# A decode kernel with cached attention and a dense branch: weights on 128 partitions, keys loaded three pieces and transposed one piece ahead, last values in four loads, sums in PSUM

## The chip, the cores and the metric

One core of one Trainium2 chip. The metric is the device time of one execution in microseconds (us), the median of several runs; lower is better. The page of a profile shows one execution. Engines: TensorE (PE, matmuls; PEld, weight loads), VectorE (DVE), ScalarE (ACT), GpSimd (POOL), SyncE (SP, which issues the loads), and 16 DMA engines. In the built programs each of the five engines has a queue of instructions of its own.

## The reference

Two tokens (batch 2, one position, D = 448). x is normalised; one branch is attention over the last 4,096 positions of a cache (16 query heads, 8 key heads, head size 256), the other a dense layer with the mish function; both are added to x.

```python
xn = layernorm(x)
q = (xn @ wq)                                   # wq [448, 4096], 16 heads of 256
s = einsum("bhqd,bhkd->bhqk", q, k[last 4096]) * 256 ** -0.5
o = einsum("bhqk,bhkd->bhqd", softmax(s), v[last 4096])
out = x + o @ wo + mish(xn @ w1 + b1) @ w2      # wo [4096, 448], w1 [448, 1792], w2 [1792, 448]
```

The data are 67.1 MB of keys and values and 10.6 MB of weights, all in bf16, 77.67 MB together.

## The kernel before

The work is cut into 32 pieces: 8 key heads, 2 batch entries, 2 halves of the positions. A piece needs 1 MB of keys and 1 MB of values. For each piece VectorE transposes the keys (kt, read as four-byte words), TensorE makes the scores with a block-diagonal q (8 matmuls), ScalarE takes the exponential and its sum (rs), VectorE transposes the result (pT), TensorE multiplies by the values (32 small matmuls into o). After two pieces den sums rs over the partitions, rec is 1/den, oT is o times rec; after four, psA collects oT times wo.

```python
def scores(s):
    kt = kt_pool.tile([P, TH * Dh], BF16, tag="kt", name="kt")          # bufs=2
    nc.vector.transpose(out=kt[:].bitcast(FP32), in_=k_t.pop(s)[:].bitcast(FP32))
    ...                                            # 8 matmuls, then Exp into p, sum into rs
def values(s):
    nc.vector.transpose(out=pT[:], in_=p_t.pop(s)[:])
    ...                                            # 32 matmuls into o; after the second half:
    ...                                            # den <- rs, rec <- 1/den, oT <- o * rec
for s in range(NSTEP + 1):
    if s + 2 < NSTEP: load_k(s + 2)
    if s + 1 < NSTEP: load_v(s + 1)                # every fourth also loads a wo
    ...
    if s < NSTEP: scores(s)
    if s >= 1:    values(s - 1)
```

wq and w1 lie on 112 partitions (448 = 4 x 112), wq in two loads. The framework in which the kernel is written orders the instructions of each engine itself when the program is built. **The queues need not have the order of the source**, and the order of a built program can be listed.

The softmax here doesn't subtract the row's maximum and nothing guards it: scores larger than these inputs give would overflow.

Of the kernel before, what the change touches and what calls it, by code (L numbers as in the profile page):

```python
# [9 lines left out]
ALU = mybir.AluOpType  # L10
# [7 lines left out]
def kernel(  # L18
# [29 lines left out]
    NS = 4  # L48
    PD = D // NS
    NF = F // P  # L50
# [3 lines left out]
    assert Sq == 1 and D % NS == 0 and PD <= P and F % P == 0  # L54
# [8 lines left out]
    kt_pool = ctx.enter_context(tc.tile_pool(name="kt", bufs=2))  # L63
# [11 lines left out]
    b1_sb = consts.tile([P, NF], BF16)  # L75
    nc.scalar.dma_start(out=b1_sb[:, :], in_=B_b1.rearrange("(q c) -> q c", q=P))

    wq_sb = weights.tile([PD, NS, HqDh], BF16)
    wq_in = A_wq.rearrange("(p s) n -> p s n", s=NS)
    NG = 2  # L80
    HG = Hq // NG
    GW = HG * Dh
    for g in range(NG):
        nc.sync.dma_start(
            out=wq_sb[:, :, g * GW : (g + 1) * GW], in_=wq_in[:, :, g * GW : (g + 1) * GW]
        )
# [20 lines left out]
    for i in range(NW):  # L107
# [17 lines left out]
    xn_bf = consts.tile([Bsz, D], BF16)  # L125
    nc.vector.tensor_scalar(  # L126
        out=xn_bf[:],
        in0=x_bf[:],
        scalar1=mv[:, 0:1],
        scalar2=rstd[:],  # L130
        op0=ALU.subtract,
        op1=ALU.mult,
    )
    xnT_ps = ps_m.tile([P, NS, Bsz], BF16, tag="m", name="xnT_ps")
    xn_v = xn_bf[:, :].rearrange("b (p s) -> b s p", s=NS)
    for s in range(NS):
        nc.tensor.transpose(xnT_ps[0:PD, s, :], xn_v[:, s, :], ident[0:Bsz, 0:Bsz])  # L137
    xnT = consts.tile([PD, NS, Bsz], BF16)
    nc.vector.tensor_copy(out=xnT[:], in_=xnT_ps[0:PD, :, :])


    qrep = consts.tile([P, NB, Hq, NE, Bsz], BF16)
    wq_v = wq_sb[:, :, :].rearrange("p s (h m e) -> p s h e m", h=Hq, e=NE)

    def project(g):
        qT_ps = ps_m.tile([P, HG, NE, Bsz], FP32, tag="m", name="qT_ps")
        for hh in range(HG):
            for e in range(NE):
                for s in range(NS):
                    nc.tensor.matmul(  # L150
                        qT_ps[:, hh, e, :],
                        lhsT=wq_v[:, s, g * HG + hh, e, :],
                        rhs=xnT[:, s, :],
                        start=(s == 0),
                        stop=(s == NS - 1),
                    )
        qT = small.tile([P, HG * NE * Bsz], BF16, tag="qT", name="qT")
        nc.vector.tensor_copy(out=qT[:], in_=qT_ps[:].rearrange("p h e b -> p (h e b)"))  # L158
        qr_ps = ps_m.tile([P, NB, HG * NE * Bsz], FP32, tag="m", name="qr_ps")
        for b4 in range(NB):  # L160
            nc.tensor.matmul(
                qr_ps[:, b4, :], lhsT=spread[:, b4, :], rhs=qT[:], start=True, stop=True
            )
        nc.vector.tensor_copy(
            out=qrep[:, :, g * HG : (g + 1) * HG, :, :].rearrange("p n h e b -> p n (h e b)"),
            in_=qr_ps[:],
        )
# [3 lines left out]
    def build_q(i):  # L171
        kvh, b = heads[i]
        t = qdiag[i % NW]
        tv = t[:].rearrange("p (n e) c -> p n e c", e=NE)
        for j in range(NQ):
            rows = slice(j * Q, (j + 1) * Q)
            for e in range(NE):
                nc.gpsimd.tensor_copy(  # L178
                    out=tv[rows, :, e, j * Q : j * Q + rep],
                    in_=qrep[rows, :, kvh * rep : (kvh + 1) * rep, e, b],  # L180
                )


    w1_sb = weights.tile([PD, NS, F], BF16)
    w2_sb = weights.tile([P, NF, D], BF16)
    xb = consts.tile([Bsz, D], FP32)
    act_bf = consts.tile([P, NF, Bsz], BF16)

    def load_dense():
        nc.sync.dma_start(out=w1_sb[:], in_=B_w1.rearrange("(p s) n -> p s n", s=NS))  # L190
        nc.sync.dma_start(out=w2_sb[:], in_=B_w2.rearrange("(q c) d -> q c d", q=P))

    def dense_in():
        w1_v = w1_sb[:].rearrange("p s (q c) -> p s c q", c=NF)
        hT_ps = ps_m.tile([P, NF, Bsz], FP32, tag="m", name="hT_ps")
        for c in range(NF):
            for s in range(NS):
                nc.tensor.matmul(  # L198
                    hT_ps[:, c, :],
                    lhsT=w1_v[:, s, c, :],  # L200
                    rhs=xnT[:, s, :],
                    start=(s == 0),
                    stop=(s == NS - 1),
                )
        h_sb = consts.tile([P, NF, Bsz], FP32, name="h_sb")
        nc.vector.tensor_tensor(
            out=h_sb[:],
            in0=hT_ps[:],
            in1=b1_sb[:].unsqueeze(2).to_broadcast([P, NF, Bsz]),
            op=ALU.add,  # L210
        )
        u_sb = consts.tile([P, NF, Bsz], FP32, name="u_sb")
        nc.scalar.activation(out=u_sb[:], in_=h_sb[:], func=ACT.Exp)
        t_sb = consts.tile([P, NF, Bsz], FP32, name="t_sb")
# [3 lines left out]
        den = consts.tile([P, NF, Bsz], FP32, name="den_sb")  # L218
# [7 lines left out]
    def dense_out():  # L226
        psB = ps_m.tile([Bsz, D], FP32, tag="m", name="psB")
        for c in range(NF):
            nc.tensor.matmul(  # L229
                psB[:, :],  # L230
                lhsT=act_bf[:, c, :],
                rhs=w2_sb[:, c, :],
                start=(c == 0),
                stop=(c == NF - 1),
            )
        nc.vector.tensor_tensor(out=xb[:], in0=psB[:, :], in1=x_bf[:], op=ALU.add)
# [3 lines left out]
    k_t, v_t, p_t, wo_t = {}, {}, {}, {}  # L240
    psA = ps_a.tile([Bsz, D], FP32)
# [10 lines left out]
    def load_v(s):  # L252
# [4 lines left out]
        nc.sync.dma_start(out=t[:], in_=vin[:, half * TH : (half + 1) * TH, :])  # L257
        v_t[s] = t
        if half == NH - 1 and b == Bsz - 1:
            w = wo_pool.tile([P, rep, ND * D], BF16, tag="wo", name="wo")  # L260
            r0 = kvh * rep * Dh
            nc.sync.dma_start(
                out=w[:],
                in_=A_wo[r0 : r0 + rep * Dh, :].rearrange("(h p c) d -> p h (c d)", h=rep, p=P),
            )
            wo_t[kvh] = w

    def scores(s):
        i = s // NH
        kt = kt_pool.tile([P, TH * Dh], BF16, tag="kt", name="kt")  # L270
        nc.vector.transpose(out=kt[:].bitcast(FP32), in_=k_t.pop(s)[:].bitcast(FP32))  # L271
        ktv = kt[:].rearrange("p (t n c e) -> p n e t c", t=TH, n=NB, e=NE)
# [22 lines left out]
    def values(s):  # L295
# [7 lines left out]
        po = state["o", i]  # L303
        v = v_t.pop(s)
# [13 lines left out]
        rs = state.pop(("rs", i))  # L318
        den = ps_den.tile([P, rep], FP32, tag="den", name="den")
        for n in range(NH):  # L320
            nc.tensor.matmul(  # L321
                den[:],
                lhsT=rs[:, n : n + 1].to_broadcast([P, P]),
                rhs=hsel[:],
                start=(n == 0),
                stop=(n == NH - 1),
            )
        rec = small.tile([P, rep], FP32, tag="rec", name="rec")
        nc.vector.reciprocal(out=rec[:], in_=den[:])  # L329
# [12 lines left out]
        for h in range(rep):  # L342
            for c in range(ND):
# [4 lines left out]
                    start=(kvh == 0 and h == 0 and c == 0),  # L348
                    stop=(kvh == Hkv - 1 and h == rep - 1 and c == ND - 1),
                )  # L350

    load_k(0)
    load_k(1)
    load_v(0)
    project(0)
    build_q(0)
    build_q(1)
    for s in range(NSTEP + 1):
        if s + 2 < NSTEP:
            load_k(s + 2)  # L360
        if s + 1 < NSTEP:
            load_v(s + 1)
        if s == 3:
            load_dense()
# [46 lines left out]
```

## Time and profile before

| | before |
|---|---|
| median, range | 211.82 us, 209.85 to 212.22 (4 runs) |
| span of the profiled run | 211.8 us |
| TensorE, VectorE, ScalarE busy | 70%, 49%, 12% |
| read from memory | 77.67 MB, 367 GB/s over the span |

The prediction below shows the slices, the stretches and the end. Two more views. First the chain of work that ended last, summed by engine:

```profile
DMA 64%; PE 24%; DVE 9%; issue 1%; ACT 0%; SPq 0%; ACTq 0%
```

Second, two pieces in steady state from the timeline (start, duration, engine, line, operation, result and operands, count, and in brackets how long the engine had stood idle and what ended it):

```profile
133.92 0.70 DVE L299 STREAM_TRANSPOSE pT<-p 128x512 bf16<-128x512 bf16 x1
134.54 2.27 DVE L271 STREAM_TRANSPOSE kt<-k 128x2048 f32<-128x2048 f32 x1
136.87 3.48 PE L276 MATMUL sc<-kt,qdiag 128*128 128x512 bf16 x8 [2.69 <-DVE kt L271]
137.24 2.31 DVE L271 STREAM_TRANSPOSE kt<-k 128x2048 f32<-128x2048 f32 x1 [0.43 <-DMA k<-in_A_k_cache_dram]
...
141.37 1.89 PE L276 MATMUL sc<-kt,qdiag 128*128 128x512 bf16 x8
...
144.78 2.27 DVE L271 STREAM_TRANSPOSE kt<-k 128x2048 f32<-128x2048 f32 x1
```

VectorE does two key transposes in a row. The first waits behind pT, and its scores wait for it; the second is already done when its scores come. Those follow other work without a wait and took 1.89 us at a granted clock of 1.00; the eight that had waited 2.69 us took 3.48 us at a mean of 0.54. Two pieces take 144.78 - 134.54 = 10.2 us.

### The profile page before, as it was taken

Reading aid. Unit: us, or ns where it says so; the run is one execution under the profiler, and the core shown is the slowest. Engines: PE = TensorE matmul, PEld = TensorE weight load, DVE = VectorE, ACT = ScalarE, POOL = GpSimd, SP = SyncE. Lnnn points to the kernel's source line nnn. Section 1 sums busy time; section 2 is a strip of 40 time slices with the busy share of each in tenths; the row PEclk is TensorE's granted clock in tenths of the full one; section 3 lists DMA queues with packets and bytes.
Section 4 is the critical chain, followed back from the end, with each engine's and each line's share of the span. In section 5 each row is a group of like instructions: output and inputs, shape, how many; then the busy total and the mean of one; then the engine's idle time right before and its main releaser. Section 6 shows DMA issues by size and latency. Waiting matters only on the chain.

```text
span 211.8 us, 3784 instructions
## 1 busy us (share of the span) xinstructions
PE 148.2 (70%) x1586; PEld 80.4 (38%) x1586; DVE 103.9 (49%) x134; ACT 25.1 (12%) x68; POOL 26.7 (13%) x138
## 2 busy tenths in 40 slices
PE   1006486946869598858694969496949596878584
PEld 0006243513563354434343434353524343344342
DVE  5200847245124654556565555645555553656511
ACT  5000020101100111111111111111111111111110
POOL 7001520200200020112020202020202020000000
PEclk9999997678555967696969797978888857696966
DMA  5999999999999999999999999999999999999500
GB/s 152 281 278 381 416 421 421 408 342 227 330 409 421 411 418 421 421 404 422 422 415 411 420 415 421 409 419 419 421 407 419 416 421 412 421 416 420 215 7 0
DMA packets 12760, 77.90 MB, mean 368 GB/s; under 512 B 1364, under 2 KB 3416, under 8 KB 4312
## 3 DMA queue, kind: packets, MB, share of 16 engines
q1 hardware_dynamic: 12596, 77.67, 93.7%
q8 instruction: 12, 0.20, 0.4%
q10 hardware_dynamic: 148, 0.01, 0.1%
q14 instruction: 4, 0.03, 0.0%
HBM read 77.67 MB, written 0.00 MB: 367 GB/s over the span
## 4 chain that ended last, share of the span: by engine, by line
DMA 64%; PE 24%; DVE 9%; issue 1%; ACT 0%; SPq 0%; ACTq 0%
DMA k<-in_A_k_cache_dram 30%; DMA v<-in_A_v_cache_dram 29%; PE sc L276 15%; DVE kt L271 6%; DMA wq_sb<-in_A_wq_dram 5%; PE o L308 4%; PE psB L229 3%; DVE pT L299 2%; PE den L321 1%; PE psA L344 1%; DVE oT L333 0%; DVE res L379 0%; ACT p L286 0%; SPq L249 0%; DVE den_sb L222 0%
## 5 line engine op out<-in xcount | busy, mean ns | idle before, releaser
L276 PE MATMUL sc<-kt,qdiag 128*128 128x512 bf16 x256 | 91.0, 517 | 38.7 <-DVE kt L271 38.1
L271 DVE STREAM_TRANSPOSE kt<-k 128x2048 f32<-128x2048 f32 x32 | 72.8, 2285 | 10.3 <-DMA k<-in_A_k_cache_dram 10.1
L276 PEld LDWEIGHTS <-qdiag 128*128 128x128 bf16 x256 | 29.3, 123 | 82.4 <-issue 38.1
L178 POOL COPY qdiag<-qrep 32x8 bf16<-32x8 bf16 x128 | 22.9, 184 | 146.3 <-PE sc L276 116.2
L286 ACT ACTIVATE p<-sc 128x512 bf16<-128x512 f32 x32 | 19.1, 597 | 174.0 <-PE sc L276 174.0
L299 DVE STREAM_TRANSPOSE pT<-p 128x512 bf16<-128x512 bf16 x32 | 22.5, 704 | 31.6 <-ACT p L286 31.6
L308 PEld LDWEIGHTS <-v 128*128 128x128 bf16 x1024 | 31.7, 99 | 13.3 <-issue 10.3
L308 PE MATMUL o<-pT,v 128*128 128x2 bf16 x1024 | 30.6, 164 | 0.4 <-DVE rec L329 0.4
L333 DVE TENSOR_TENSOR oT<-o,rec 128x4 bf16<-128x4 f32 x16 | 2.6, 165 | 38.5 <-PE o L308 38.5
L321 PE MATMUL den<-hsel,rs 128*128 128x2 f32 x64 | 12.9, 273 | 0.1
L150 PE MATMUL qT_ps<-xnT,wq_sb 112*128 112x2 bf16 x128 | 3.9, 165 | 12.2 <-DMA wq_sb<-in_A_wq_dram 12.2
L321 PEld LDWEIGHTS den<-hsel,rs 128*128 128x128 f32 x64 | 10.2, 202 | 4.6 <-issue 2.7
L344 PE MATMUL psA<-wo,oT 128*2 128x448 bf16 x32 | 7.6, 362 | 2.1 <-DVE oT L333 2.1
L150 PEld LDWEIGHTS <-wq_sb 112*128 112x128 bf16 x128 | 3.6, 104 | 12.3 <-DMA wq_sb<-in_A_wq_dram 12.3
L158 DVE CAST qT<-qT_ps 128x32 bf16<-128x32 f32 x2 | 0.4, 190 | 13.9 <-PE qT_ps L150 13.9
L229 PE MATMUL psB<-w_sb,act_bf 128*2 128x448 bf16 x14 | 5.4, 574 | 1.8 <-DVE act_bf L224 1.8
L286 ACT ACTIVATION_READ_ACCUMULATOR p<-sc 128x1 f32 x32 | 6.2, 194 | 0.0
L198 PE MATMUL hT_ps<-xnT,w_sb 112*128 112x2 bf16 x56 | 3.5, 198 | 0.6 <-DMA w_sb<-in_B_w_dram 0.6
L137 PE MATMUL xnT_ps<-ident,xn_bf 2*112 2x2 bf16 x4 | 0.6, 243 | 4.6 <-DVE xn_bf L126 4.6
L198 PEld LDWEIGHTS <-w_sb 112*128 112x128 bf16 x56 | 3.4, 157 | 0.7 <-DMA w_sb<-in_B_w_dram 0.7
L344 PEld LDWEIGHTS <-oT 128*2 128x2 bf16 x32 | 2.0, 82 | 4.5 <-DVE oT L333 2.8
L229 PEld LDWEIGHTS <-act_bf 128*2 128x2 bf16 x14 | 1.6, 120 | 4.8 <-issue 3.0
(34 smaller groups left out, 18.5 us busy)
## 6 DMA issues: line engine op xcount, KB each, us to landing
k<-in_A_k_cache_dram SPq DMA_DIRECT2D x32, 1024.0 KB, 18.6
v<-in_A_v_cache_dram SPq DMA_DIRECT2D x32, 1024.0 KB, 18.6
wq_sb<-in_A_wq_dram SPq DMA_DIRECT2D x2, 1792.0 KB, 13.1
wo<-in_A_wo_dram SPq DMA_DIRECT2D x8, 448.0 KB, 18.6
w_sb<-in_B_w_dram SPq DMA_DIRECT2D x2, 1568.0 KB, 27.5
x_bf<-in_A_x_dram ACTq DMA_DIRECT2D x1, 1.8 KB
b_sb<-in_B_b_dram ACTq DMA_DIRECT2D x1, 3.5 KB, 5.8
out_dram<-res SPq DMA_DIRECT2D x1, 1.8 KB
```

What stands on the lines that cost most here:

```text
L150: nc.tensor.matmul(qT_ps[:, hh, e, :], lhsT=wq_v[:, s, g * HG + hh, e, :], rhs=xnT[:, s, :], start=(s == 0), stop=(s == NS - 1),)
L178: nc.gpsimd.tensor_copy(out=tv[rows, :, e, j * Q : j * Q + rep], in_=qrep[rows, :, kvh * rep : (kvh + 1) * rep, e, b],)
L198: nc.tensor.matmul(hT_ps[:, c, :], lhsT=w1_v[:, s, c, :], rhs=xnT[:, s, :], start=(s == 0), stop=(s == NS - 1),)
L229: nc.tensor.matmul(psB[:, :], lhsT=act_bf[:, c, :], rhs=w2_sb[:, c, :], start=(c == 0), stop=(c == NF - 1),)
L271: nc.vector.transpose(out=kt[:].bitcast(FP32), in_=k_t.pop(s)[:].bitcast(FP32))
L276: nc.tensor.matmul(psc[:], lhsT=qdiag[i % NW][:, n * NE + e, :], rhs=ktv[:, n, e, :, :], start=(n == 0 and e == 0), stop=(n == NB - 1 and ...
L286: nc.scalar.activation(out=p_sb[:], in_=psc[:].rearrange("p t c -> p (t c)"), func=ACT.Exp, scale=scale, accum_out=state["rs", i][:, s % N ...
L299: nc.vector.transpose(out=pT[:], in_=p_t.pop(s)[:])
L308: nc.tensor.matmul(po[:, c, :], lhsT=vv[:, t, c, :], rhs=pTv[:, t, 0:rep], start=(half == 0 and t == 0 and c == 0), stop=(half == NH - 1 a ...
L321: nc.tensor.matmul(den[:], lhsT=rs[:, n : n + 1].to_broadcast([P, P]), rhs=hsel[:], start=(n == 0), stop=(n == NH - 1),)
L333: nc.vector.tensor_tensor(out=oT[:, :, :, b], in0=po[:], in1=rec[:].unsqueeze(1).to_broadcast([P, ND, rep]), op=ALU.mult,)
L344: nc.tensor.matmul(psA[:, :], lhsT=oT[:, c, h, :], rhs=w[:, h, c * D : (c + 1) * D], start=(kvh == 0 and h == 0 and c == 0), stop=(kvh == ...
```

## The change

Its intent: fill the holes in the loads by using all 128 partitions for wq and w1 (each row of the matrix cut into two half-rows, 896 = 7 x 128), let TensorE never wait for kt by transposing keys one piece ahead, shorten the end by loading the last values in four parts and wo early, and gather x and the dense branch in the PSUM tile of the attention.

```diff
-    wq_sb = weights.tile([PD, NS, HqDh], BF16)            # PD = 112
+    wq_sb = weights.tile([P, NS, HW], BF16)               # P = 128, NS = 7, HW = half a row
+    wq_in = A_wq.rearrange("r (x n) -> (r x) n", x=NX).rearrange("(p s) n -> p s n", s=NS)
...                                                         # w1 alike; xs holds xn, split by half-row
-    kt_pool = ... bufs=2
+    kt_pool = ... bufs=3
...
+        n = LAST if s == NSTEP - 1 else 1                  # load_v: LAST = 4
+        for u in range(n): ...
+    def turn(s):                                           # the key transpose, taken out of scores
+        kt = kt_pool.tile([P, TH * Dh], BF16, tag="kt", name="kt")
+        nc.vector.transpose(out=kt[:].bitcast(FP32), in_=k_t.pop(s)[:].bitcast(FP32))
...                                                         # values: den and rec moved ahead of the 32 matmuls
+    KA, VA = 3, 1
+    for s in range(KA): load_k(s)
+    load_wo(0)
...
+    turn(0)
     for s in range(NSTEP + 1):
-        if s + 2 < NSTEP:
-            load_k(s + 2)
+        if s + KA < NSTEP:
+            load_k(s + KA)
...
+        if s + 1 < NSTEP:
+            turn(s + 1)
         if s < NSTEP:
             scores(s)
         if s >= 1:
             values(s - 1)
...
-    nc.vector.tensor_tensor(out=res[:], in0=psA[:, :], in1=xb[:], op=ALU.add)
+    nc.vector.tensor_copy(out=res[:, 0 : D // 2], in_=psA[:, 0 : D // 2])
+    nc.scalar.copy(out=res[:, D // 2 : D], in_=psA[:, D // 2 : D])
```

More of the change, by code (lines that the diff above doesn't have):

```diff
@@ L47 @@
     TH = T // NH
-    NS = 4
-    PD = D // NS
-    NF = F // P
+    NX = 2
+    NS = D * NX // P
+    HW = HqDh // NX
+    HF = F // NX
+    HH = Hq // NX
+    NF = HF // P
     ND = Dh // P
@@ L53 @@
     NE = 2
-    assert Sq == 1 and D % NS == 0 and PD <= P and F % P == 0
+    assert Sq == 1 and D * NX == NS * P and NS % 2 == 1 and HF % P == 0 and Hq % NX == 0
     assert TH * Q <= 512 and NB * NE * Q == Dh and ND == 2
@@ L62 @@
     v_pool = ctx.enter_context(tc.tile_pool(name="vv", bufs=6))
-    kt_pool = ctx.enter_context(tc.tile_pool(name="kt", bufs=2))
+    kt_pool = ctx.enter_context(tc.tile_pool(name="kt", bufs=3))
     p_pool = ctx.enter_context(tc.tile_pool(name="pp", bufs=2))
@@ L74 @@
     nc.scalar.dma_start(out=x_bf[:, :], in_=A_x.flatten_outer_dims())
-    b1_sb = consts.tile([P, NF], BF16)
-    nc.scalar.dma_start(out=b1_sb[:, :], in_=B_b1.rearrange("(q c) -> q c", q=P))
-    wq_sb = weights.tile([PD, NS, HqDh], BF16)
-    wq_in = A_wq.rearrange("(p s) n -> p s n", s=NS)
-    NG = 2
-    HG = Hq // NG
-    GW = HG * Dh
-    for g in range(NG):
-        nc.sync.dma_start(
-            out=wq_sb[:, :, g * GW : (g + 1) * GW], in_=wq_in[:, :, g * GW : (g + 1) * GW]
-        )
+    b1_sb = consts.tile([1, F], BF16)
+    nc.scalar.dma_start(out=b1_sb[:, :], in_=B_b1.rearrange("(o f) -> o f", o=1))
+    wq_sb = weights.tile([P, NS, HW], BF16)
+    wq_in = A_wq.rearrange("r (x n) -> (r x) n", x=NX).rearrange("(p s) n -> p s n", s=NS)
+    SC = NS // 2 + 1
+    nc.sync.dma_start(out=wq_sb[:, 0:SC, :], in_=wq_in[:, 0:SC, :])
+    nc.sync.dma_start(out=wq_sb[:, SC:NS, :], in_=wq_in[:, SC:NS, :])
     ident = consts.tile([P, P], BF16)
@@ L124 @@
     nc.vector.reciprocal(out=rstd[:], in_=rstd[:])
-    xn_bf = consts.tile([Bsz, D], BF16)
-    nc.vector.tensor_scalar(
-        out=xn_bf[:],
-        in0=x_bf[:],
-        scalar1=mv[:, 0:1],
-        scalar2=rstd[:],
-        op0=ALU.subtract,
-        op1=ALU.mult,
-    )
-    xnT_ps = ps_m.tile([P, NS, Bsz], BF16, tag="m", name="xnT_ps")
-    xn_v = xn_bf[:, :].rearrange("b (p s) -> b s p", s=NS)
-    for s in range(NS):
-        nc.tensor.transpose(xnT_ps[0:PD, s, :], xn_v[:, s, :], ident[0:Bsz, 0:Bsz])
@@ L138 @@
-    xnT = consts.tile([PD, NS, Bsz], BF16)
-    nc.vector.tensor_copy(out=xnT[:], in_=xnT_ps[0:PD, :, :])
-    qrep = consts.tile([P, NB, Hq, NE, Bsz], BF16)
-    wq_v = wq_sb[:, :, :].rearrange("p s (h m e) -> p s h e m", h=Hq, e=NE)
-    def project(g):
-        qT_ps = ps_m.tile([P, HG, NE, Bsz], FP32, tag="m", name="qT_ps")
-        for hh in range(HG):
+    xn_bf = consts.tile([Bsz, NS, P // 2, 2], BF16)
+    x_all = x_bf[:, :]
+    for r in range(2):
+        n = (NS + 1 - r) // 2
+        nc.vector.tensor_scalar(
+            out=xn_bf[:, r : NS : 2, :, :],
+            in0=bass.AP(
+                x_all.tensor,
+                x_all.offset,
+                [list(x_all.ap[0]), [1, n], [NS, P // 2], [(NS + r) // 2, 2]],
+            ),
+            scalar1=mv[:, 0:1],
+            scalar2=rstd[:],
+            op0=ALU.subtract,
+            op1=ALU.mult,
+        )
@@ new lines @@
+    xnT_ps = ps_m.tile([P, NS, Bsz], BF16, tag="m", name="xnT_ps")
+    for s in range(NS):
+        nc.tensor.transpose(
+            xnT_ps[:, s, :],
+            xn_bf[:, s, :, :].rearrange("b u o -> b (u o)"),
+            ident[0:Bsz, 0:Bsz],
+        )
+    odd = consts.tile([P, 2], FP32)
+    nc.vector.tensor_reduce(
+        out=odd[:],
+        in_=ident[:].rearrange("p (u o) -> p o u", o=2),
+        axis=AXIS.X,
+        op=ALU.add,
+    )
+    xs = consts.tile([P, NS, NX, Bsz], BF16)
@@ new lines @@
+    for par in range(2):
+        for x in range(NX):
+            which = (par + x) % 2
+            nc.vector.tensor_scalar(
+                out=xs[:, par : NS : 2, x, :],
+                in0=xnT_ps[:, par : NS : 2, :],
+                scalar1=odd[:, which : which + 1],
+                scalar2=None,
+                op0=ALU.mult,
+            )
+    ones = consts.tile([1, Bsz], BF16)
+    nc.vector.memset(ones[:], 1.0)
+    psA = ps_a.tile([Bsz, D], FP32)
+    nc.tensor.matmul(
+        psA[:, :],
+        lhsT=ident[0:Bsz, 0:Bsz],
+        rhs=x_bf[:, :],
+        start=True,
+        stop=False,
+        skip_group_check=True,
+    )
@@ L148, in project @@
+    qrep = consts.tile([P, NB, HH, NE, NX, Bsz], BF16)
+    wq_v = wq_sb[:, :, :].rearrange("p s (h m e) -> p s h e m", h=HH, e=NE)
+    def project():
+        qT_ps = ps_m.tile([P, HH, NE, NX * Bsz], FP32, tag="m", name="qT_ps")
+        for hh in range(HH):
             for e in range(NE):
@@ L151, in project @@
                         qT_ps[:, hh, e, :],
-                        lhsT=wq_v[:, s, g * HG + hh, e, :],
-                        rhs=xnT[:, s, :],
+                        lhsT=wq_v[:, s, hh, e, :],
+                        rhs=xs[:, s, :, :].rearrange("p x b -> p (x b)"),
                         start=(s == 0),
@@ L156, in project @@
                     )
-        qT = small.tile([P, HG * NE * Bsz], BF16, tag="qT", name="qT")
-        nc.vector.tensor_copy(out=qT[:], in_=qT_ps[:].rearrange("p h e b -> p (h e b)"))
-        qr_ps = ps_m.tile([P, NB, HG * NE * Bsz], FP32, tag="m", name="qr_ps")
+        n = HH * NE * NX * Bsz
+        qT = consts.tile([P, n], BF16, name="qT")
+        nc.vector.tensor_copy(out=qT[:], in_=qT_ps[:].rearrange("p h e c -> p (h e c)"))
+        qr_ps = ps_m.tile([P, NB, n], FP32, tag="m", name="qr_ps")
         for b4 in range(NB):
@@ L164, in project @@
         nc.vector.tensor_copy(
-            out=qrep[:, :, g * HG : (g + 1) * HG, :, :].rearrange("p n h e b -> p n (h e b)"),
-            in_=qr_ps[:],
+            out=qrep[:].rearrange("p n h e x b -> p n (h e x b)"), in_=qr_ps[:]
         )
@@ L172, in build_q @@
         kvh, b = heads[i]
+        x, h0 = divmod(kvh * rep, HH)
         t = qdiag[i % NW]
@@ L179, in build_q @@
                     out=tv[rows, :, e, j * Q : j * Q + rep],
-                    in_=qrep[rows, :, kvh * rep : (kvh + 1) * rep, e, b],
+                    in_=qrep[rows, :, h0 : h0 + rep, e, x, b],
                 )
-    w1_sb = weights.tile([PD, NS, F], BF16)
-    w2_sb = weights.tile([P, NF, D], BF16)
-    xb = consts.tile([Bsz, D], FP32)
-    act_bf = consts.tile([P, NF, Bsz], BF16)
+    w1_sb = weights.tile([P, NS, HF], BF16)
+    w2_sb = weights.tile([P, NX, NF, D], BF16)
+    act_bf = consts.tile([P, NF, NX, Bsz], BF16)
     def load_dense():
-        nc.sync.dma_start(out=w1_sb[:], in_=B_w1.rearrange("(p s) n -> p s n", s=NS))
-        nc.sync.dma_start(out=w2_sb[:], in_=B_w2.rearrange("(q c) d -> q c d", q=P))
+        nc.sync.dma_start(
+            out=w1_sb[:],
+            in_=B_w1.rearrange("r (x n) -> (r x) n", x=NX).rearrange("(p s) n -> p s n", s=NS),
+        )
+        nc.sync.dma_start(
+            out=w2_sb[:], in_=B_w2.rearrange("(x q c) d -> q x c d", x=NX, q=P)
+        )
     def dense_in():
         w1_v = w1_sb[:].rearrange("p s (q c) -> p s c q", c=NF)
-        hT_ps = ps_m.tile([P, NF, Bsz], FP32, tag="m", name="hT_ps")
+        b1_v = b1_sb[:].rearrange("o (x q c) -> o x c q", x=NX, c=NF)
+        hT_ps = ps_m.tile([P, NF, NX, Bsz], FP32, tag="m", name="hT_ps")
         for c in range(NF):
@@ L198, in dense_in @@
                 nc.tensor.matmul(
-                    hT_ps[:, c, :],
+                    hT_ps[:, c, :, :].rearrange("p x b -> p (x b)"),
                     lhsT=w1_v[:, s, c, :],
-                    rhs=xnT[:, s, :],
+                    rhs=xs[:, s, :, :].rearrange("p x b -> p (x b)"),
                     start=(s == 0),
-                    stop=(s == NS - 1),
-                )
-        h_sb = consts.tile([P, NF, Bsz], FP32, name="h_sb")
-        nc.vector.tensor_tensor(
-            out=h_sb[:],
-            in0=hT_ps[:],
-            in1=b1_sb[:].unsqueeze(2).to_broadcast([P, NF, Bsz]),
-            op=ALU.add,
-        )
-        u_sb = consts.tile([P, NF, Bsz], FP32, name="u_sb")
+                    stop=False,
+                    skip_group_check=True,
+                )
+            for x in range(NX):
+                nc.tensor.matmul(
+                    hT_ps[:, c, x, :],
+                    lhsT=b1_v[:, x, c, :],
+                    rhs=ones[:, :],
+                    start=False,
+                    stop=True,
+                    skip_group_check=True,
+                )
+        shape = [P, NF, NX, Bsz]
+        h_sb = consts.tile(shape, FP32, name="h_sb")
+        nc.vector.tensor_copy(out=h_sb[:], in_=hT_ps[:])
+        u_sb = consts.tile(shape, FP32, name="u_sb")
         nc.scalar.activation(out=u_sb[:], in_=h_sb[:], func=ACT.Exp)
-        t_sb = consts.tile([P, NF, Bsz], FP32, name="t_sb")
+        t_sb = consts.tile(shape, FP32, name="t_sb")
         nc.vector.scalar_tensor_tensor(
@@ L217, in dense_in @@
         )
-        den = consts.tile([P, NF, Bsz], FP32, name="den_sb")
+        den = consts.tile(shape, FP32, name="den_sb")
         nc.vector.tensor_scalar(
@@ L226, in dense_out @@
     def dense_out():
-        psB = ps_m.tile([Bsz, D], FP32, tag="m", name="psB")
-        for c in range(NF):
-            nc.tensor.matmul(
-                psB[:, :],
-                lhsT=act_bf[:, c, :],
-                rhs=w2_sb[:, c, :],
-                start=(c == 0),
-                stop=(c == NF - 1),
-            )
-        nc.vector.tensor_tensor(out=xb[:], in0=psB[:, :], in1=x_bf[:], op=ALU.add)
+        for x in range(NX):
+            for c in range(NF):
+                nc.tensor.matmul(
+                    psA[:, :],
+                    lhsT=act_bf[:, c, x, :],
+                    rhs=w2_sb[:, x, c, :],
+                    start=False,
+                    stop=False,
+                    skip_group_check=True,
+                )
     NSTEP = len(heads) * NH
-    k_t, v_t, p_t, wo_t = {}, {}, {}, {}
-    psA = ps_a.tile([Bsz, D], FP32)
+    LAST = 4
+    k_t, kt_t, v_t, p_t, wo_t = {}, {}, {}, {}, {}
     state = {}
@@ L256, in load_v, with load_wo @@
         vin = A_v_cache[b, kvh, s0:Sk, :].rearrange("(p t) d -> p t d", p=P)
-        nc.sync.dma_start(out=t[:], in_=vin[:, half * TH : (half + 1) * TH, :])
-        v_t[s] = t
-        if half == NH - 1 and b == Bsz - 1:
-            w = wo_pool.tile([P, rep, ND * D], BF16, tag="wo", name="wo")
-            r0 = kvh * rep * Dh
-            nc.sync.dma_start(
-                out=w[:],
-                in_=A_wo[r0 : r0 + rep * Dh, :].rearrange("(h p c) d -> p h (c d)", h=rep, p=P),
-            )
-            wo_t[kvh] = w
+        n = LAST if s == NSTEP - 1 else 1
+        for u in range(n):
+            lo, hi = u * TH // n, (u + 1) * TH // n
+            nc.sync.dma_start(
+                out=t[:, lo:hi, :], in_=vin[:, half * TH + lo : half * TH + hi, :]
+            )
+        v_t[s] = t
+    def load_wo(kvh):
+        w = wo_pool.tile([P, rep, ND * D], BF16, tag="wo", name="wo")
+        r0 = kvh * rep * Dh
+        nc.sync.dma_start(
+            out=w[:],
+            in_=A_wo[r0 : r0 + rep * Dh, :].rearrange("(h p c) d -> p h (c d)", h=rep, p=P),
+        )
+        wo_t[kvh] = w
+    def turn(s):
+        kt = kt_pool.tile([P, TH * Dh], BF16, tag="kt", name="kt")
+        nc.vector.transpose(out=kt[:].bitcast(FP32), in_=k_t.pop(s)[:].bitcast(FP32))
+        kt_t[s] = kt
     def scores(s):
         i = s // NH
-        kt = kt_pool.tile([P, TH * Dh], BF16, tag="kt", name="kt")
-        nc.vector.transpose(out=kt[:].bitcast(FP32), in_=k_t.pop(s)[:].bitcast(FP32))
-        ktv = kt[:].rearrange("p (t n c e) -> p n e t c", t=TH, n=NB, e=NE)
+        ktv = kt_t.pop(s)[:].rearrange("p (t n c e) -> p n e t c", t=TH, n=NB, e=NE)
         psc = ps_sc.tile([P, TH, Q], FP32, tag="sc", name="sc")
@@ L303, in values @@
         po = state["o", i]
+        if half == NH - 1:
+            rs = state.pop(("rs", i))
+            den = ps_den.tile([P, rep], FP32, tag="den", name="den")
+            for n in range(NH):
+                nc.tensor.matmul(
+                    den[:],
+                    lhsT=rs[:, n : n + 1].to_broadcast([P, P]),
+                    rhs=hsel[:],
+                    start=(n == 0),
+                    stop=(n == NH - 1),
+                )
+            rec = small.tile([P, rep], FP32, tag="rec", name="rec")
+            nc.vector.reciprocal(out=rec[:], in_=den[:])
         v = v_t.pop(s)
@@ L317, in values @@
             return
-        rs = state.pop(("rs", i))
-        den = ps_den.tile([P, rep], FP32, tag="den", name="den")
-        for n in range(NH):
-            nc.tensor.matmul(
-                den[:],
-                lhsT=rs[:, n : n + 1].to_broadcast([P, P]),
-                rhs=hsel[:],
-                start=(n == 0),
-                stop=(n == NH - 1),
-            )
-        rec = small.tile([P, rep], FP32, tag="rec", name="rec")
-        nc.vector.reciprocal(out=rec[:], in_=den[:])
         if b == 0:
@@ L347, in values @@
                     rhs=w[:, h, c * D : (c + 1) * D],
-                    start=(kvh == 0 and h == 0 and c == 0),
+                    start=False,
                     stop=(kvh == Hkv - 1 and h == rep - 1 and c == ND - 1),
+                    skip_group_check=True,
                 )
-    load_k(0)
-    load_k(1)
-    load_v(0)
-    project(0)
+    KA, VA = 3, 1
+    for s in range(KA):
+        load_k(s)
+    load_wo(0)
+    for s in range(VA):
+        load_v(s)
+    project()
     build_q(0)
     build_q(1)
+    turn(0)
     for s in range(NSTEP + 1):
-        if s + 2 < NSTEP:
-            load_k(s + 2)
-        if s + 1 < NSTEP:
-            load_v(s + 1)
+        if s + KA < NSTEP:
+            load_k(s + KA)
+        if s + VA < NSTEP:
+            load_v(s + VA)
         if s == 3:
             load_dense()
+        if s % (NH * Bsz) == 0 and s // (NH * Bsz) + 1 < Hkv:
+            load_wo(s // (NH * Bsz) + 1)
         if s % NH == 0 and 0 < s < NSTEP - NH:
             build_q(s // NH + 1)
+        if s + 1 < NSTEP:
+            turn(s + 1)
         if s < NSTEP:
@@ L370 @@
             values(s - 1)
-        if s == 2:
-            project(1)
         if s == 9:
```

## The prediction

The sum came to 9.1 + 0.9 + 3.8 = 13.8 us, thus a span of 198.0. But for the 9.1 only measured rates are left (272 and 239 GB/s on 112 partitions against about 416); that 128 partitions would load at K's rate, and that "equal shares" are worth 0.9, were the author's estimates.

> **What bounds the kernel now.** I read the page's slices first, then the stretches, then the chain and the timeline of the end.
>
> The slices of the page:
>
> ```profile
> DMA  5999999999999999999999999999999999999500
> GB/s 152 281 278 381 416 421 421 408 342 227 330 409 421 411 418 421 421 404 422 422 415 411 420 415 421 409 419 419 421 407 419 416 421 412 421 416 420 215 7 0
> ```
>
> One slice is 5.3 us. The 16 DMA engines are busy from slice 2 to slice 37, so transfers bound the kernel. But busy does not mean fast: about 416 GB/s is normal here, and there are two holes at full business, at the start (281, 278) and in slices 9 to 11 (342, 227, 330). After slice 38 nothing moves for some 9 us. The stretches give the same with sharper edges (the last two columns are the DMA share and GB/s):
>
> ```profile
> 2.00:16.00 14.00, 0.76 (x5) 0.59 (x5) 4.19 (x25) 2.56 (x3) 2.44 (x3) 1.00 1.01 272
> 16.00:22.00 6.00, 3.91 (x135) 3.79 (x136) 0.67 (x3) 0.00 (x0) 1.40 (x10) 1.00 1.00 386
> 45.00:53.00 8.00, 6.01 (x48) 2.77 (x49) 2.98 (x4) 0.69 (x2) 0.00 (x0) 0.71 1.03 239
> 53.00:58.00 5.00, 4.36 (x44) 2.46 (x42) 0.81 (x2) 0.69 (x2) 1.48 (x8) 0.50 0.97 326
> 70.00:190.00 120.00, 93.27 (x984) 49.80 (x982) 67.73 (x69) 15.81 (x46) 14.74 (x80) 0.80 1.01 416
> 198.00:203.00 5.00, 2.31 (x30) 1.30 (x27) 2.97 (x3) 0.53 (x2) 0.00 (x0) 0.85 0.22 81
> 203.00:212.00 9.00, 5.48 (x76) 2.89 (x74) 1.54 (x4) 0.69 (x2) 0.00 (x0) 0.69 0.00 0
> ```
>
> The first hole is wq (two loads of 1,792 KB), the second w1 (1,568 KB) and then w2: w1 and wq are the only large loads that go to 112 partitions. Between 70 and 190 us TensorE is busy 93.27 of 120 us (78%) and VectorE 67.73 (56%), so neither is the bound in steady state. From 198 to 203 us only stragglers arrive: single-microsecond stretches show 237, 70, 53, 25, 20 GB/s, and one engine alone is about 416/16 = 26 GB/s. So one or two DMA engines run some 4 us behind the others. From 203.0 us to the end at 211.8, 8.8 us, there is only computation. Its last part in the timeline:
>
> ```profile
> 198.70 0.70 DVE L299 STREAM_TRANSPOSE pT<-p 128x512 bf16<-128x512 bf16 x1
> 199.32 2.27 DVE L271 STREAM_TRANSPOSE kt<-k 128x2048 f32<-128x2048 f32 x1
> 201.65 3.52 PE L276 MATMUL sc<-kt,qdiag 128*128 128x512 bf16 x8 [2.69 <-DVE kt L271]
> 207.88 1.21 PE L344 MATMUL psA<-wo,oT 128*2 128x448 bf16 x4 [0.26 <-DVE oT L333]
> 209.13 0.61 DVE L379 TENSOR_TENSOR res<-psA,xb 2x448 bf16<-2x448 f32 x1 [1.30 <-PE psA L344]
> 209.77 0.32 SPq L380 DMA_DIRECT2D out_dram<-res  x1
> ```
>
> The key transpose of the last piece stands behind pT of the piece before, scores wait 2.69 us for it, and the eight score matmuls then take 3.52 us, where eight that follow other work take 1.90. In the chain of waits the last transfer is a k at 166.08; from there on transposes, scores and values follow one another with 10.3 us for two pieces (178.75 to 189.07 from one kt to the same kt). Transfers need 2 x 2.21 MB / 0.416 = 10.6 us for two pieces (K, V and a quarter of wo each). So the serial computation is almost as slow as the loads, and it stands behind the last of them.
>
> [...] wq's packets of 4,096 B take 240 ns on average and w1's of 14,336 B 977 ns (17 and 15 B/ns an engine), K and V's of 8,192 B 313 ns in the median (26 B/ns). [...]
>
> **The change part by part.**
>
> Weights on 128 partitions. The bytes stay (77.67 MB). Between 2 and 22 us 14 x 272 + 6 x 386 = 6,124 KB moved; at 416 that is 14.7 us, so 5.3 us were lost, of which some 0.7 is the ramp (102 GB/s from 2 to 3 us) and remains: 4.6. Between 45 and 58 us 8 x 239 + 5 x 326 = 3,542 KB moved, 8.5 us at 416, so 4.5 lost. All of it lies on the path, as the engines are busy everywhere after it: **9.1 us** if the new loads run at K's rate.
>
> Stragglers. The packets of wo show how far apart the engines are: some 3.4 us from its first packet to its last for the first wo (about 40 us), 5.4 after w1, 6.9 at the end; 1.2 of each is its own work (16 packets of 75 ns). One engine falls back by about 2 us over the w1 stage. I give **0.9 us**, half of it, to equal shares. The last load should then land at 203.0 - 9.1 - 0.9 = 193.0 us.
>
> The tail after it. Before 8.8 us. K is loaded three pieces ahead and transposed one ahead, wo before it is needed, so what comes last is v of the last piece, in four quarters, each of 256 KB. After the last quarter: 8 of the 32 value matmuls (0.94 us), 0.24, plus 0.16 latency; oT 0.17 and gaps 0.06; four psA matmuls 1.2; half of the result copied (612 ns for 448 columns, 165 ns for an operation of 4, thus 1.0 ns a column: 0.39 for 224, ScalarE alike beside it); issue to end of the output 211.8 - 209.77 = 2.05. Sum 4.3. Does TensorE keep up? The last k lands three V loads before the end, 7.5 us; its transpose is done 5 us before. TensorE then does the values of piece 29 (v lands 5.0 before the end), scores of 31 (1.9 to 3.5 us), values of 30 (v 2.5 us before the end). The exponential (0.60 + 0.19) and pT (0.71) of piece 31 follow the scores. At full clock all fits; at half clock values of 31 start about 1.5 us late. I add the half: **5.0 us**, so 3.8 saved.
>
> What is added: 112 + 49 weight loads instead of 128 + 56, 14 bias matmuls, 3 transposes more, one 448-column matmul, some seven small VectorE operations (0.15 to 0.6 us each, before 11 us, when VectorE is busy 0.80 of 10 us). xb's addition (0.61) and the first hole's second project leave. All of it lies beside loads: 0 on the path. Key transposes cost the same 2.27 us each; moving them takes the wait from scores (38.1 us of TensorE idle ended by kt), which is worth nothing while loads bound, only at the end.
>
> Sum: 9.1 + 0.9 + 3.8 = 13.8 us; span 198.0, and about the same for the time (before 211.8 and 212.1).
>
> **The rivals.**
>
> First: the holes come from something else than the partitions (long rows, memory pages). For it: w2 has 128 partitions and its packets of 12,544 B still took 658 ns on average, where K's rate gives 479. Against: they get faster within the stage, 855 early and about 500 late, as if only w1's leftovers disturbed them, and K packets right after wq (15.3 to 17.2 us) also take 450 to 600. Then only the tail would gain: 208. If only w2 stays slow, +1.
>
> Second: with faster loads the computation becomes the bound. For it: 10.3 against 10.6 us for two pieces. Against: that cycle contains kt (2.2 us a pair on the path) and goes. Even with all scores at half clock TensorE has 2 x (3.56 + 0.95) + 0.38 + 0.92 = 10.3 us, [...]. If the clock stays low to the end: 200 to 202.
>
> Third: the lagging engine gets no better, or worse (the 12 instruction packets of about 1.07 us each stay): 199 to 201. If the lag vanishes: 194.5.
>
> **Range and chances.** The spread of the three runs before (209.85 to 212.22) is some 1 us each way, the lag 2, the rate of the new loads 1.5, the tail 1: 194.5 to 202.5 around 198. The 2% line is 207.9; only the first rival in full reaches it, for which I leave 4%.
>
> **What would show it.** Right: no slice between 3 and 36 under some 400 GB/s; wq done by about 11 to 12 us, first scores before 17 us; stragglers end at 192 to 194; scores no longer idle behind kt; from the last v to the end 4.3 to 6 us. Wrong: slices of 230 to 340 while wq or w1 load with all partitions; TensorE busy through with loads waiting on buffers; or a tail above 7 us.

## The result, and the profile after

| | before | after |
|---|---|---|
| median | 211.82 us (4 runs) | 271.58 us (4 runs, 269.08 to 273.65) |
| span, mean granted clock | 211.8 us, 0.80 | 267.3 us, 0.66 |
| TensorE, VectorE busy | 148.2, 103.9 us | 167.8, 103.8 us |
| ratio of the fast runs | | 1.274, 95% interval 1.260 to 1.288 |

A ratio here and below is the mean time of one kernel's fast runs over that of the other's in the same rounds, so it is not quite the ratio of the medians. A run more than 1.5% above the fastest of its kernel counts as slow and is left out (two of the four of the changed kernel). The changed kernel is 27% slower; the prediction had said 6.5% faster.

The slices of the page after (6.7 us each):

```profile
PEclk9999855557575586579575557568565557559556
DMA  7999999999999999699887966699886914400000
GB/s 278 417 420 418 417 418 427 415 412 421 423 412 422 418 400 343 264 337 362 312 316 265 363 215 223 264 348 350 310 283 237 362 67 157 157 2 0 0 2 0
```

The stretches after (start and end, length, then busy us and number of instructions of PE, PEld, DVE, ACT and POOL, the granted clock, DMA share, GB/s):

```profile
2.00:16.00 14.00, 4.63 (x124) 3.78 (x124) 5.03 (x32) 2.44 (x3) 2.44 (x3) 1.00 0.96 400
45.00:53.00 8.00, 5.35 (x44) 2.40 (x44) 3.07 (x3) 0.24 (x2) 0.00 (x0) 0.50 1.00 412
70.00:190.00 120.00, 78.95 (x700) 35.73 (x700) 47.34 (x47) 10.31 (x30) 11.82 (x64) 0.64 0.89 333
190.00:260.00 70.00, 45.26 (x387) 20.23 (x386) 27.26 (x27) 6.25 (x19) 2.96 (x16) 0.60 0.38 137
```

The holes are gone as predicted: 400 GB/s from 2 to 16 us (before 272) and 412 from 45 to 53 (before 239). But from about 95 us on the loads fall to 333 and then 137 GB/s, and the last 30 us have none. Between 70 and 190 us TensorE is busy 78.95 us (before 93.27) and VectorE 47.34 (before 67.73): both do less in the same time. So nothing is overloaded, and everything waits. The chain of work that ended last says where:

```profile
PE 58%; DVE 25%; issue 8%; DMA 4%; ACT 3%; SPq 0%; ACTq 0%; DVEq 0%
PE sc L339 39%; DVE kt L330 20%; PE o L384 10%; DMA wq_sb<-in_A_wq_dram 4%; PE psA L408 4%; DVE pT L362 4%; ACT p L349 3%; PE den L371 1%; PE psA L283 1%; PE hT_ps L246 1%; PE qT_ps L192 1%; PE hT_ps L255 1%; DVE rec L379 0%; DVE qrep L207 0%; SPq L86 0%
```

Transfers made up 64% of that chain before and 4% after. What the issue of loads waited for, before (first line) and after, from the view of waits of the DMA queue (us in total, times, longest):

```profile
SPq L249 <- DMA v<-in_A_v_cache_dram: 55.8, 25, 3.7
```

```profile
SPq L314 <- PE o L384: 66.2, 22, 9.1
SPq L303 <- DVE kt L330: 53.4, 11, 5.4
```

Before, a load waited for an earlier load; after, loads wait for the values and the key transposes to free their buffers. The computation is late, not the data. One piece of it in the timeline:

```profile
161.71 0.71 DVE L362 STREAM_TRANSPOSE pT<-p 128x512 bf16<-128x512 bf16 x1 [5.19 <-ACT p L349]
...
162.35 2.27 DVE L330 STREAM_TRANSPOSE kt<-k 128x2048 f32<-128x2048 f32 x1
...
164.68 1.89 PE L339 MATMUL sc<-kt,qdiag 128*128 128x512 bf16 x4 [2.56 <-DVE kt L330]
...
166.36 1.03 PE L384 MATMUL o<-pT,v 128*128 128x2 bf16 x32
...
167.25 1.87 PE L339 MATMUL sc<-kt,qdiag 128*128 128x512 bf16 x4
...
169.16 0.60 ACT L349 ACTIVATE p<-sc 128x512 bf16<-128x512 f32 x1 [7.48 <-PE sc L339]
...
169.88 0.71 DVE L362 STREAM_TRANSPOSE pT<-p 128x512 bf16<-128x512 bf16 x1 [2.28 <-ACT p L349]
```

This is a closed ring: pT, then kt of the next piece, its scores, its exponential, its pT. This turn of it takes 169.88 - 161.71 = 8.17 us; over the whole run the 32 pT start from 22.9 to 260.7 us, 7.67 us apart in the mean. VectorE stands idle 5.19 us before pT, waiting for the exponential, while the keys for kt have long landed (this piece's at 124.9 us, 37 us before its kt). In the groups of the page (busy us, mean ns, idle us before and what ended it) no kt ever waited for anything at the head of the queue, and pT's wait for the exponential makes 104.8 us:

```profile
L330 DVE STREAM_TRANSPOSE kt<-k 128x2048 f32<-128x2048 f32 x32 | 72.3, 2275 | 0.0
L362 DVE STREAM_TRANSPOSE pT<-p 128x512 bf16<-128x512 bf16 x32 | 22.7, 711 | 107.0 <-ACT p L349 104.8
```

So a ready kt stood for 5.19 us behind a pT that was not ready. In both traces VectorE starts pT, kt, rec and oT of pieces 7 to 14 in the order of the built programs, listed next.

The order of VectorE's queue in the built programs, with K3 for the key transpose of piece 3 and p3 for its pT, r for rec, o for oT (pieces 7 to 14; not a profile, but a listing of the programs):

```text
source of after   ... K8 p6 K9 p7 K10 p8 K11 p9 K12 p10 K13 p11 ...
built, before     p7 r o p8 K9 K10 p9 r o p10 K11 K12 p11 r o p12 K13 K14
built, after      p7 r K8 p8 K9 o p9 K10 r p10 K11 o p11 r K12 K13 p12 o p13 K14
```

In the program of after, 24 of the 32 key transposes stand behind the pT of the piece before, in that of before 17; the traces show the same order and the same counts. "One piece ahead" is not there at all. To see what turn(s + 1) does, I built, without running them, the kernel before with it (and kt with three buffers), and the kernel after without it: in both pairs all five queues have the very same order. Taking the transpose out of scores and writing it earlier changed no order.

### The profile page after: what moved, and what is told of

It is laid out like the page before. It is cut to its first block, busy times and chain, and to the rows that moved or that the text cites. A ratio compares the mean times of both kernels' runs of the same rounds, so it can differ in the third digit from the quotient of the medians.

```text
span 267.3 us, 3777 instructions
## 1 busy us (share of the span) xinstructions
PE 167.8 (63%) x1577; PEld 80.4 (30%) x1577; DVE 103.8 (39%) x137; ACT 25.4 (10%) x69; POOL 26.8 (10%) x138
## 4 chain that ended last, share of the span: by engine, by line
PE 58%; DVE 25%; issue 8%; DMA 4%; ACT 3%; SPq 0%; ACTq 0%; DVEq 0%
PE sc L339 39%; DVE kt L330 20%; PE o L384 10%; DMA wq_sb<-in_A_wq_dram 4%; PE psA L408 4%; DVE pT L362 4%; ACT p L349 3%; PE den L371 1%; PE psA L283 1%; PE hT_ps L246 1%; PE qT_ps L192 1%; PE hT_ps L255 1%; DVE rec L379 0%; DVE qrep L207 0%; SPq L86 0%
## 5 line engine op out<-in xcount | busy, mean ns | idle before, releaser
L339 PE MATMUL sc<-kt,qdiag 128*128 128x512 bf16 x256 | 109.1, 569 | 62.5 <-DVE kt L330 47.3
L362 DVE STREAM_TRANSPOSE pT<-p 128x512 bf16<-128x512 bf16 x32 | 22.7, 711 | 107.0 <-ACT p L349 104.8
L339 PEld LDWEIGHTS <-qdiag 128*128 128x128 bf16 x256 | 26.2, 122 | 100.2 <-issue 68.2
L371 PEld LDWEIGHTS den<-hsel,rs 128*128 128x128 f32 x64 | 12.5, 242 | 45.8 <-ACT p L349 45.6
L408 PE MATMUL psA<-wo,oT 128*2 128x448 bf16 x32 | 10.8, 478 | 0.3 <-DVE oT L397 0.3
L192 PE MATMUL qT_ps<-xs,wq_sb 128*128 128x4 bf16 x112 | 3.3, 166 | 5.8 <-DMA wq_sb<-in_A_wq_dram 5.8
L192 PEld LDWEIGHTS <-wq_sb 128*128 128x128 bf16 x112 | 3.1, 104 | 6.4 <-DMA wq_sb<-in_A_wq_dram 6.4
L283 PE MATMUL psA<-w_sb,act_bf 128*2 128x448 bf16 x14 | 3.7, 413 | 0.0
L246 PE MATMUL hT_ps<-xs,w_sb 128*128 128x4 bf16 x49 | 3.7, 195 | 0.0
L246 PEld LDWEIGHTS <-w_sb 128*128 128x128 bf16 x49 | 3.2, 151 | 0.1
L110 POOL MEMSET qdiag<- 128x1024 bf16 x3 | 2.7, 951 | 0.0
(40 smaller groups left out, 20.3 us busy)
## 6 DMA issues: line engine op xcount, KB each, us to landing
wq_sb<-in_A_wq_dram SPq DMA_DIRECT2D x1, 1536.0 KB, 10.9
```

Of the source, the lines that this page charges most:

```text
L110: nc.gpsimd.memset(t[:], 0.0)
L192: nc.tensor.matmul(qT_ps[:, hh, e, :], lhsT=wq_v[:, s, hh, e, :], rhs=xs[:, s, :, :].rearrange("p x b -> p (x b)"), start=(s == 0), stop=( ...
L246: nc.tensor.matmul(hT_ps[:, c, :, :].rearrange("p x b -> p (x b)"), lhsT=w1_v[:, s, c, :], rhs=xs[:, s, :, :].rearrange("p x b -> p (x b)" ...
L283: nc.tensor.matmul(psA[:, :], lhsT=act_bf[:, c, x, :], rhs=w2_sb[:, x, c, :], start=False, stop=False, skip_group_check=True,)
L339: nc.tensor.matmul(psc[:], lhsT=qdiag[i % NW][:, n * NE + e, :], rhs=ktv[:, n, e, :, :], start=(n == 0 and e == 0), stop=(n == NB - 1 and ...
L371: nc.tensor.matmul(den[:], lhsT=rs[:, n : n + 1].to_broadcast([P, P]), rhs=hsel[:], start=(n == 0), stop=(n == NH - 1),)
```

## The experiments

Theory: the 60 us come from VectorE's queue, in which kt stands behind pT (or behind rec, see below), so that the pieces run one after another. Rivals: TensorE's queue, which in the built program has den directly behind its own scores and the 32 values in the middle of the scores; the half clock; the early key loads as such; another part of the change. Ten kernels ran, all gave correct results. "Pinned" means an order of issue added at build, without any wait.

**1. VectorE's pT pinned behind the key transpose one piece ahead.**

```diff
-        nc.vector.transpose(out=pT[:], in_=p_t.pop(s)[:])
+        with tc.issue_after(state["turn"].ins):           # the kt traced last: piece s + 2 of this pT
+            nc.vector.transpose(out=pT[:], in_=p_t.pop(s)[:])
```

> The changed kernel with one order added: pT of piece s-1 stands behind the key transpose of piece s+1 in VectorE's queue, as the source has it; TensorE's queue stays about as built (den of a piece directly behind its own scores, values in the middle of the scores). Theory (VectorE's queue: every key transpose stands behind the pT of the piece before, so pT, kt, scores, exponential form one serial ring of 8.2 us a piece): the ring opens, TensorE then needs 4.2 to 6.2 us a piece and the loads 5.3, so 195 to 215 us. Rival (TensorE's queue, which waits for the exponential at den and splits the scores): unchanged there, so over 250 us.

Measured: 240.38 us (235.27 to 241.27; one run counts as fast, so no ratio). Both expectations missed, the time lies between them: the one fast run, 235.27 us, has 24 of some 58 us of loss left. The profile is of a slow run (240.04 us). VectorE's wait for rec shows what is left, and the timeline how:

```profile
DVE rec L382 <- PE den L374: 46.4, 15, 5.0
```

```profile
150.11 0.59 PE L374 MATMUL den<-hsel,rs 128*128 128x2 f32 x2 [0.78 <-ACT p L351]
150.73 0.17 DVE L382 RECIPROCAL rec<-den 128x2 f32<-128x2 f32 x1 [2.93 <-PE den L374]
150.82 2.29 DVE L330 STREAM_TRANSPOSE kt<-k 128x2048 f32<-128x2048 f32 x1
```

Every second piece has a rec, which stood before kt. It waits for den, den for the exponential, and kt for rec: the same ring with another member. (oT's wait for o is longer still, 57.4 us in all; it falls to 20.3 in run 5, where rec alone is pinned in addition.) Whether rec, or TensorE's order, keeps the rest is what run 5 decides.

**2. The mirror: TensorE's queue as the source has it, VectorE's in the bad order.** Every matmul of the loop pinned behind the one before it in the source, den after the values; pT traced before kt, and kt pinned behind it.

> The mirror of the first run: TensorE's queue put into the order of the source (eight scores, 32 values, den after them), and every key transpose held behind the pT of the piece before, as in the changed kernel. Theory (VectorE's queue): the ring stays, 0.64 pT + 2.33 kt + 3.6 scores at half clock + 0.8 exponential = 7.4 us a piece, 32 pieces and 22 us of start and end: 250 to 270 us. Rival (TensorE's queue): under 220 us.

Measured: 273.35 us, ratio 1.295 (1.287 to 1.302). The ring stays, as the theory has it, though 3 us above its range; the source's order on TensorE does not heal it (31 of the 32 key transposes stand behind a pT here). The mean granted clock of the four runs was 0.636 to 0.727 and their times 272.78 to 273.70 us, 273.36 at the lowest clock and 273.35 at the highest: the mean clock does not decide the time. Inside a ring the half clock does lengthen a turn: in the lines above eight scores take 1.89 + 1.87 us at a granted 0.50, in the kernel before 1.89 at 1.00, so some 1.9 of the 8.17 us by an estimate from these lines. No run separates that share.

**3. The kernel before with keys three pieces ahead, nothing else.**

```diff
+    load_k(2)
-        if s + 2 < NSTEP:
-            load_k(s + 2)
+        if s + 3 < NSTEP:
+            load_k(s + 3)
```

> The kernel before with a single edit: keys are loaded three pieces ahead instead of two; weights, transposes in the source, values, sums as before. In the built program this alone moves most key transposes behind the pT of the piece before. Theory (the load order changes VectorE's queue, and that alone costs): 240 to 275 us. Rival (some other part of the change, the weights, the PSUM sums or the early transposes, costs the time): 205 to 214 us, as before.

Measured: 274.58 us, ratio 1.300 (1.293 to 1.308). One number in the loads makes the whole loss. In this program 23 key transposes stand behind the pT of the piece before. Its four pieces take 30.9 us (161.36 - 130.50, from one pair of transposes to the next).

**4. The changed kernel with both queues in the order of the source.** Runs 1's pin, den after the values, all matmuls of the loop in order.

> The changed kernel with both queues in the order of the source: key transposes truly one piece ahead, and on TensorE eight scores, 32 values, den after the values. Theory: loads are the bound again and the prediction's sum applies, 193 to 203 us, and not slower than the first run. Rival (something in the change other than the order costs time as well, say the half clock): over 205 us.

Measured: 198.83 us, ratio 0.943 (0.938 to 0.948). The prediction's 198.0 comes true once its order does.

**5. Run 1 and rec pinned too, TensorE's queue left to the scheduler.**

```diff
-            nc.vector.reciprocal(out=rec[:], in_=den[:])
+            with tc.issue_after(state["turn"].ins):
+                nc.vector.reciprocal(out=rec[:], in_=den[:])
```

> The first run with one more order added: rec, too, stands behind the key transpose that is one piece ahead. VectorE's queue is then the same as in the fourth run (198.8 us); TensorE's queue keeps the built order (scores split by values, den directly behind scores). Theory (the 40 us that the first run kept come from rec: it waits for den, den for the exponential, and the next kt stands behind rec, so the ring stays closed for one piece of two): 196 to 206 us. Rival (TensorE's own order costs them): 225 to 240 us as the first run.

Measured: 198.07 us, ratio 0.937 (0.931 to 0.943). Scores are still split by the values here, and den still stands directly behind scores; that costs nothing measurable beside run 4. VectorE's queue carries the loss. One thing moved with the pin: the two den matmuls that run 1 has between the scores of the two halves now stand behind those of the second, so run 5 is not run 1 with VectorE's queue alone changed. The slices and VectorE's longest wait of this run:

```profile
GB/s 217 429 422 413 422 414 426 419 426 414 414 414 424 416 419 413 420 422 422 413 412 424 421 419 411 426 412 422 412 418 422 426 409 417 422 417 424 410 171 0
```

```profile
DVE kt L330 <- DMA k<-in_A_k_cache_dram: 47.2, 27, 3.5
```

kt now waits for its keys, and loads run at over 400 GB/s from the second slice to the 38th: this kernel is bound by its loads.

**6. The weights' part alone,** nothing pinned: the changed kernel with keys two ahead, wo, last values and transposes as before.

> Only the weights as half-rows with the sums in PSUM (and den ahead of the values in the source); keys two pieces ahead, wo, last values and key transposes as in the kernel before; nothing is pinned. In its built order three of four key transposes stand behind the pT of the piece before, in the kernel before two of four. Theory (the time follows VectorE's order): about 3 x 7.8 + 3 = 26 us for four pieces, so 215 to 240 us, although the loads of weights are faster. Rival (faster weight loads carry through): 197 to 204 us.

Measured: 230.99 us, ratio 1.082 (1.073 to 1.092). Even the good part alone loses, since here too the order changed: 22 key transposes stand behind a pT. Four pieces take 27.1 us (157.79 - 130.69). Run 3 has nearly as many but 30.9 us; in its trace the values (1.03 us, as in after at a granted 0.50; 0.94 in before at 1.00) run between the scores and so lie inside the ring, here they follow them. So TensorE's order seems to lengthen a ring that exists (no run changes it alone within one); it doesn't make one: in the traces all 1,376 scores, values, den and psA matmuls of the loop stand in the very same order in run 6 and in the kernel before, and only run 6 lost. No run pins this kernel itself; run 8, with the same weights, keys and transposes further ahead and the good order, takes 198.76 us.

**7. The kernel before with the good order,** keys three and transposes one ahead, both queues pinned; weights on 112 partitions. **8. Run 4 with the last values in one load and wo where it was.** The two differ in the weights and the PSUM sums alone.

> The kernel before with keys three pieces ahead, transposes one piece ahead and both queues held in the order of the source; weights on 112 partitions, wo and last values as before. Against the fourth run (198.8) it lacks the weights' part. Prediction's term (9.1 us for weights on 128 partitions, 0.9 for the lag): 207 to 211 us. Rival (the holes are hidden or come from elsewhere): 199 to 203 us.

> The fourth run with the last values in one load again and wo loaded where the kernel before loads it (the last wo behind the last v). Whole v needs 0.94 us of matmuls after landing instead of 0.24, but it lands 1.1 us earlier as wo's 459 KB come after it, and wo is needed only after the values. Expected within 1 us of 198.8: 198 to 200 us. If the four loads carry the tail: over 201 us.

Measured: 209.61 us (ratio 0.993, 0.987 to 0.998, thus the same within 2%) and 198.76 us (ratio 0.940, 0.934 to 0.947). The weights and sums are worth 209.61 - 198.76 = 10.9 us; the last bytes land between 200 and 201 us in run 7 and between 190 and 191 in run 8, so nearly all of it lies in the loads. The four loads and the early wo are worth nothing that can be told (run 4 had 198.83). The stretches of run 7 and then of run 8:

```profile
2.00:16.00 14.00, 0.76 (x5) 0.59 (x5) 4.19 (x25) 2.56 (x3) 2.44 (x3) 1.00 1.02 266
45.00:53.00 8.00, 6.83 (x54) 2.95 (x55) 3.24 (x4) 0.69 (x2) 1.47 (x8) 0.79 1.06 322
53.00:58.00 5.00, 0.83 (x8) 0.34 (x7) 0.00 (x0) 0.69 (x2) 0.00 (x0) 0.91 0.95 285
```

```profile
2.00:16.00 14.00, 4.63 (x124) 3.78 (x124) 5.85 (x32) 2.42 (x3) 2.44 (x3) 1.00 0.95 402
45.00:58.00 13.00, 7.49 (x113) 6.10 (x110) 4.16 (x8) 1.21 (x5) 1.07 (x6) 0.71 1.00 413
```

**9. The kernel before with nothing but VectorE's bad order.** pT traced before kt, kt pinned behind it; the order of the loads is exactly that of before. TensorE's queue, which the scheduler orders anew, moved a little with it.

> The kernel before, its loads in their built order untouched (keys two ahead), with VectorE's queue alone held so that every key transpose stands behind the pT of the piece before. Theory (that order by itself makes the time): 7.4 to 8.2 us a piece, 32 pieces and 22 us: 255 to 285 us. Rival (the early key loads of the changed kernel, not the queue, cost the time): 208 to 215 us.

Measured: 269.32 us, ratio 1.275 (1.266 to 1.284). The early key loads are not needed to lose the time; the order of the queue is enough.

**10. Run 5 with one copy of the result.**

> The fifth run (198.1) with the result copied by one VectorE instruction again, 0.61 us, instead of two halves which in the trace follow one another (0.38 on VectorE, then 0.34 on ScalarE, 0.77 in all). Expected 0.1 to 0.2 us better, thus not to be told from 198: 197.5 to 198.5.

Measured: 197.76 us, ratio 0.937 (0.931 to 0.943), not to be told from run 5. It is the fastest median here and beats both kernels.

What remains open is why the scheduler chooses as it does. That the order of loads changes it is shown (run 3); that it weighs by an estimate of its own of when keys land, and takes a pT that it thinks ready sooner, is only argued.

## Why the prediction was wrong

Its bound and its holes hold once the order is right; one step carried everything and failed. The step is **"K is loaded three pieces ahead and transposed one ahead"** in the part on the tail, used again in the second rival: **"that cycle contains kt (2.2 us a pair on the path) and goes"**. It took the order of the source for the order of the queue. The trace of before already contradicted this: there VectorE does kt, kt, pT, rec, oT, pT, while the source of before has kt and pT alternating. The prediction quoted a kt behind a pT from the timeline of the end and did not ask why it stood there. Runs 1, 5 and 9 put this step in its place: with the order of the source in VectorE's queue the changed kernel takes 198.1 us, with the opposite order the kernel before takes 269.3.

Point by point:

- Weights on 128 partitions, 9.1 us, and 0.9 for stragglers: their sum is right. Runs 7 and 8 give 10.9 us together with the PSUM sums, and the rates of the stretches are 402 and 413 GB/s; the 0.9 no run measures alone. The rival that blamed long rows or memory pages is out: w1's packets on 128 partitions are nearly as long as before (12,544 B against 14,336) and took 477 ns in the mean in the trace of after, against 977 before. Stretches with loads onto 112 partitions ran at 266 to 272 GB/s (wq, run 7 and before) and at 239 (w1, before); why they are slow stays open.
- The last load at 193.0 us: in run 4 the last bytes come between 190 and 191 us (37 GB/s there, 0 after), two microseconds better. The first scores came at 18.6 us there, not before 17.
- The tail of 5.0 us: mis-sized. In run 4 it is 197.2 - 191 = 6.2 us. That the span came to 197.2 us, so near to 198.0, is partly luck: the last load was 2 us early and the tail 1.2 us long. Its last lines:

```profile
191.27 0.94 PE L374 MATMUL o<-pT,v 128*128 128x2 bf16 x32 [0.74 <-DVE pT L365]
...
194.38 0.38 DVE L452 CAST res<-psA 2x224 bf16<-2x224 f32 x1 [1.31 <-PE psA L410]
194.79 0.34 ACT L453 CAST res<-psA 2x224 bf16<-2x224 f32 x1 [4.32 <-DVE res L452]
```

  All 32 values run after the last v, as pT comes late, not 8 of them; that fits the four loads gaining nothing. And the two halves of the copy, which the prediction had side by side, follow one another.
- "Worth nothing while loads bound", of the key transposes: right for the good order (run 7 is 1.7 us faster than before, 209.61 against 211.28 in the same rounds).
- The second rival, computation as the bound at 200 to 202 us at worst: the right rival with a wrong limit. In the ring TensorE, though behind, stood idle before scores 24 times in after (47.3 us for kt, 15.3 for rec), and the bound is the sum of the ring, 7.67 us a piece in the mean, not the load of any engine.
- What the prediction named as a sign of error, "TensorE busy through with loads waiting on buffers", was half of what came: loads waited on buffers, but TensorE was busy only 63%.
- The clock: of the eights of scores that it names, the one after a wait of 2.69 us took 3.52 us at a mean granted clock of 0.53, the other 1.90 at 1.00. When the clock falls the traces do not settle. In the kernel before no wait of TensorE between 70 and 190 us was longer than 2.73 us, and the granted clock there fell to 0.50 eleven times (mean 0.80); the eight scores at 78.14 us, which had not waited, took 3.57 us at 0.50.

## What to carry to other kernels

Where a framework orders the queues, read the order of each engine's queue in the built program (or in the trace) before reckoning with a lead that stands in the source; if the lead matters, pin it, and pin every instruction that closes the ring, as here pT and rec. An edit that touches only loads can reorder an engine that has nothing to do with loads. Busy shares don't show such a ring: look for the repeating chain of waits and add up one turn of it.
